# The last 16 channels' differences on 104 token rows, packed difference arrays, and a new order of work

## The chip, the cores and the metric

The kernel runs on one core of one Trainium2 chip. The metric is device time in microseconds (us): the median of several runs. The engines are PE (TensorE, matrix products; its weight loads are listed as PEld), DVE (VectorE), ACT (ScalarE), POOL (GpSimd) and SP (SyncE, which here only issues transfers). Each engine works through its own instructions in order and waits on semaphores.

## What is computed

A causal, dilated convolution of 15 taps over 2 sequences of 16,000 tokens with 144 channels, a gate, and a last projection:

```python
B, T, D, K = (2, 16000, 144, 15)          # x (B,T,D), w (K,D,2D), w_o (D,D), bf16
dil = 2
pad = (K - 1) * dil
xp = jnp.pad(x, ((0, 0), (pad, 0), (0, 0)))
h = jnp.einsum('btc,cd->btd', xp[:, pad:pad + T, :], w[0])
for i in range(1, K):
    off = pad - i * dil
    h = h + jnp.einsum('btc,cd->btd', xp[:, off:off + T, :], w[i])
f = h[..., :D]
g = h[..., D:]
z = jnp.tanh(f) * _sigmoid(g)
return z @ w_o
```

## The kernel before

**Windows and octets.** The tokens are cut into 16 windows of 2048 (WT), each with 32 tokens of history before it (WB = 2080). A window is worked in two octets, one for the even and one for the odd tokens (rho = 0, 1): 32 octets in all. An octet makes 8 outputs for each of 128 groups of 16 tokens. Sums of weights multiply x itself and differences of x are multiplied by single weights, so that products are shared between outputs.

**Leaves.** In an octet, A1, A2, A3, B1 and C1 are leaves: two products in common (`v` in the plan: vA1, vB ...), a copy by ACT to a second bank of PSUM (`k`: kA2, kB ...), then private products for each of two results (`p`: pA2_0, pA2_1 ...). `d` (dB_0 ...) copies a B or C result into one more bank, B2, B3, C2 and C3 add direct products. `a1s` copies A1's results to SBUF, `q` and `y` combine on DVE, `th` and `sg` are tanh and sigmoid on ACT, `m` multiplies them into z, `zt` transposes z by DMA, `g` is the output projection on PE, `po` its copy out by ACT, `ost` the store. PSUM has two banks for A, five for B and C, one for the projection.

**Differences.** From the transposed window xn (channels on partitions) DVE makes d2, d4, d8 (x at distance 2, 4, 8), d48 (of d4, at 8), d28 and d24 (of d2, at 8 and 4). Products read them with a step of 16 tokens (`st`, L246). In d8, d48 and d28 the runs that are needed alternate in sign, so each is made by two instructions, one for each sign (`sets_`, L117 to L122).

**The last 16 channels.** 144 channels are 128 and 16. For the last 16 the tokens are rearranged in DRAM (`gather`, L91: array xg, four arrays by the token's remainder modulo 4) and read back transposed with rows of 128 = 8 tokens x 16 channels that overlap (`remainder`, L101: tile rx), so that one product covers 8 tokens. DVE makes `re`, the difference of tokens 2 apart, from rx on all 128 partitions: two instructions of 2 x 513 elements a window (L125). rx serves A2 and A3, re serves B2, B3, C2, C3.

**The order.** PE, ACT, DVE and SP follow a plan written out by hand: `PLAN` lists the operations of one octet, with an offset in octets after the colon. An entry of octet n with offset a is issued in slot n + a, and within a slot in the plan's order. Entries for a window (differences, loads) come once in two octets. All transfers but the stores of results, and some at the start, are issued on SP in that order, so one that waits holds up those behind it. `late` holds operations of the first octet that are put in just before the first that needs them.

**The start and the end.** At the start 20 products of zeros run on PE, the first window and the weights are loaded (xn and the four pieces of w_all on SP; raw, the last 16 channels of w, and the gather of the first window on ACT's queue), and sums of weights are made: sm, ss, a1v, av and bc by DVE, bcv by PE with an identity matrix and a copy by ACT (`summed`, L196). s_r, ns_r, wo_p and we_r come from raw through a product with `swap`. At the end (`finish_early`, `finish`) the projections of the last three octets run, and the last z is transposed by PE.

## Time and profile before

| what | us |
|---|---|
| median of 3 runs | 342.88 (342.65 to 343.07) |
| the profiled execution | 342.56 |
| its span, first to last instruction | 340.8 |
| PE, DVE, ACT busy | 327.7, 302.0, 241.0 |
| mean granted TensorE clock | 0.99 |
| transfers | 143,110 packets, 38.32 MB |
| SP's waits for z before a transpose of it | 153.4 in 28 waits |

The profile lists each engine's busy time. A matrix product is shown with a duration of 0.286 us for 288 columns, but products overlap, so that PE's busy time is the time in which any runs. "x2" merges two neighbouring instructions into a row. Behind a row, in brackets, stands the idle time before it and what ended that.

### The profile page before, as it was taken

The numbers are of one execution on the slowest core, as the hardware profiler recorded it, in microseconds if no ns is written. First come the engines' busy times: TensorE is split into PE (matmuls) and PEld (weight loads), VectorE is DVE, ScalarE is ACT, GpSimd is POOL, SyncE is SP. The second block draws the span as 40 slices with busy tenths as digits, with TensorE's granted clock in tenths as the row PEclk, the third lists the DMA queues.
The fourth block names the chain that finished last, engine by engine and source line by source line (L and its number), as shares of the span: only waits on it lengthen the run. The fifth ranks groups of instructions, "written<-read, shape, count | busy, mean of one in ns | idle before, by whom it ended". The sixth has DMA issues, their size and how long they took to land.

```text
span 340.8 us, 7525 instructions
## 1 busy us (share of the span) xinstructions
PE 327.7 (96%) x2705; PEld 307.4 (90%) x2705; DVE 302.0 (89%) x726; ACT 241.0 (71%) x583; POOL 7.6 (2%) x22
## 2 busy tenths in 40 slices
PE   8679999999999999999999999999999999999983
PEld 3469999999999999999999999999999999999972
DVE  3889999999999999999999999998999999998662
ACT  1535787777778777777777777777777777787763
POOL 8000000000000000000000000000000000000000
PEclk9799999999999999999999999999999999999998
DMA  8872454466664465666566459657445666632313
GB/s 191 161 106 38 53 114 78 138 100 168 107 163 96 71 140 81 167 107 169 90 60 165 83 139 108 170 102 106 128 71 143 106 167 107 95 110 37 104 37 126
DMA packets 143110, 38.32 MB, mean 112 GB/s; under 512 B 138866, under 2 KB 141058, under 8 KB 143074
## 3 DMA queue, kind: packets, MB, share of 16 engines
q1 hardware_dynamic: 138286, 29.12, 49.0%
q10 hardware_dynamic: 4500, 8.66, 7.2%
q8 instruction: 21, 0.34, 0.4%
q14 instruction: 15, 0.12, 0.1%
q0 software_dynamic: 288, 0.07, 0.1%
HBM read 2.38 MB, written 10.30 MB: 37 GB/s over the span
## 4 chain that ended last, share of the span: by engine, by line
PE 92%; DMA 4%; DVE 1%; ACT 1%; issue 1%; SPq 0%; DVEq 0%; ACTq 0%
PE bc L244 57%; PE a L244 25%; PE po L369 4%; PE po L366 4%; DMA w_all<-in_w_dram 3%; DMA zt<-z 1%; SPq L88 0%; PE bc L366 0%; DVE d L122 0%; PE bc L200 0%; PE bc L369 0%; DVE q L305 0%; ACT a L270 0%; DVE re L132 0%; ACT th L332 0%
## 5 line engine op out<-in xcount | busy, mean ns | idle before, releaser
L244 PEld LDWEIGHTS <-d 128*128 128x128 bf16 x1856 | 231.8, 145 | 8.3 <-issue 2.7
L244 PE MATMUL bc<-w_all,d 128*128 128x288 bf16 x960 | 156.8, 286 | 1.9 <-DVE d L122 1.6
L327 DVE TENSOR_TENSOR y<-q,bc 128x288 f32<-128x288 f32 x256 | 113.6, 450 | 13.1 <-PE bc L244 10.4
L270 ACT COPY a<-a 128x288 f32<-128x288 f32 x96 | 36.8, 383 | 57.6 <-PE a L244 57.5
L305 DVE TENSOR_TENSOR q<-a1s,a 128x288 f32<-128x288 f32 x128 | 52.6, 451 | 13.1 <-PE a L244 11.1
L274 ACT COPY bc<-bc 128x288 f32<-128x288 f32 x128 | 50.8, 398 | 15.6 <-PE bc L244 14.6
L122 DVE TENSOR_TENSOR d<-d 128x516 bf16<-128x516 bf16 (+1 forms) x96 | 59.7, 668 | 0.0
L244 PE MATMUL a<-sm,d 128*128 128x288 bf16 x256 | 50.0, 287 | 0.8 <-ACT a L270 0.8
L244 PE MATMUL bc<-bc,d 128*128 128x288 bf16 x256 | 47.1, 286 | 0.1
L122 DVE TENSOR_TENSOR d<-xn 128x260 bf16<-128x260 bf16 (+2 forms) x64 | 42.6, 690 | 4.5 <-DMA xn<-in_x_dram 4.5
L332 ACT ACTIVATE sg<-y 128x576 bf16<-128x576 f32 x64 | 44.1, 689 | 1.0 <-DVE y L327 1.0
L332 ACT ACTIVATE th<-y 128x576 bf16<-128x576 f32 x64 | 43.7, 682 | 0.0
L359 ACT CAST o<-po 128x432 bf16<-128x432 f32 (+1 forms) x87 | 41.8, 481 | 0.8 <-PE po L369 0.8
L244 PE MATMUL bc<-wo_p,re 128*128 128x288 bf16 x128 | 36.6, 286 | 0.0
L244 PE MATMUL bc<-we_r,re 128*128 128x288 bf16 x128 | 36.6, 286 | 0.0
L339 DVE TENSOR_TENSOR z<-th,sg 128x512 bf16<-128x512 bf16 (+1 forms) x128 | 35.6, 301 | 0.0
L302 ACT COPY a1s<-a 128x288 f32<-128x288 f32 x64 | 25.9, 409 | 7.4 <-PE a L244 7.2
L369 PEld LDWEIGHTS <-zt 128*128 128x128 bf16 x256 | 22.8, 98 | 8.4
L369 PE MATMUL po<-wo_m,zt 128*128 128x144 bf16 x235 | 29.1, 226 | 0.0
L244 PEld LDWEIGHTS <-re 128*128 128x128 bf16 x256 | 28.8, 112 | 0.1
L366 PE MATMUL po<-wo_bd,zt 128*128 128x432 bf16 (+1 forms) x88 | 28.7, 326 | 0.0
L270 ACT COPY bc<-bc 128x288 f32<-128x288 f32 x64 | 25.8, 403 | 4.0 <-ACT a1s L302 2.2
(54 smaller groups left out, 228.6 us busy)
## 6 DMA issues: line engine op xcount, KB each, us to landing
out_dram<-o ACTq DMA_DIRECT2D x13, 576.0 KB
xg<-in_x_dram SPq DMA_DIRECT2D x28, 32.5 KB
w_all<-in_w_dram SPq DMA_DIRECT2D x3, 288.0 KB
out_dram<-o SPq DMA_DIRECT2D x1, 576.0 KB
zt<-z SPq DMA_TRANSPOSE x31
out_dram<-o ACTq DMA_DIRECT2D x1, 468.0 KB
out_dram<-o ACTq DMA_DIRECT2D x1, 288.0 KB
rx<-xg SPq DMA_TRANSPOSE x17
```

The lines of the kernel that those rows point to most:

```text
L122: nc.vector.tensor_tensor(out=o, in0=a, in1=b_, op=ALU.subtract)
L244: nc.tensor.matmul(ps[:, 0:D2], lhsT=l, rhs=r, start=start, stop=stop, skip_group_check=on)
L270: nc.scalar.copy(out=self.ts[1][:, 0:D2], in_=self.ts[0][:, 0:D2])
L274: nc.scalar.copy(out=self.other[i][:, 0:D2], in_=self.ts[i][:, 0:D2])
L302: nc.scalar.copy(out=self.get(cp_pool, "a1s", [P, 2, D2], F32)[:, i, :], in_=self.A1.ts[i][:, 0:D2])
L305: nc.vector.tensor_tensor(out=self.get(cp_pool, name, [P, 2, D2], F32)[:, i, :], in0=self.t["a1s"][:, i, :], in1=leaf.ts[i][:, 0:D2], op=op)
L327: nc.vector.tensor_tensor(out=y[:, k + 4 * i, :], in0=self.t[q][:, i, :], in1=ts[i][:, 0:D2], op=op)
L332: nc.scalar.activation(out=t[:], in_=self.t["y"][:, k::2, lo:lo + D], func=func)
L339: nc.vector.tensor_tensor(out=o, in0=th[:, :, lo:lo + n], in1=sg[:, :, lo:lo + n], op=ALU.mult)
L359: nc.scalar.copy(out=o, in_=a)
L366: nc.tensor.matmul(o.po[g][:, 0:n * D], lhsT=o.zt[:, 8, :], rhs=wo_bd[:, r0:r0 + n, :].rearrange("p r e -> p (r e)"), start=True, stop=False)
L369: nc.tensor.matmul(o.po[g][:, i * D:(i + 1) * D], lhsT=o.zt[:, r0 + i, :], rhs=wo_m[:], start=False, stop=i == n - 1)
```

## The change

- The last 16 channels are loaded as they lie, 20 tokens and 2 more on each of 104 partitions (`gather`, tile xt). ACT copies them (`rest`, plan entry `cr`) and DVE subtracts tokens 2 apart (`rest_diff`, `dr`), both ordered by the token's remainder modulo 4, into xs. Two transfers (`spread`, `wg`) write both to xg, and two transposes read them back as rx and re. DVE no longer makes re from rx.
- d4 and d48 are kept packed, two tokens of each four, and are read with a step of 8. The other derived arrays but d8 start two elements further on (`pad`). d8 and d28 are made by one instruction, with a zero step in one operand; d48 by two shorter-strided ones; d4 as one run.
- Half of bc (j = 0, 1) is summed on PE, with copies by ACT; DVE makes the other half. The first window's d48 comes after the third sum of weights. The first A2 uses the banks of B and C.
- The plan is another: among others d48 and d24 move from the slot before to the slot of their use, d2, d4 and d8 from two slots before to one, and the output's work (g, po) to an earlier slot.
- On ACT's queue at the start the first window's loads come ahead of raw.

```diff
 PLAN = """
-    pA3_1:0 xg:-2 sg0:1 m1a:2 d28:-1 kB:0 rx0:-1 po0:3 pB_0:0 m1b:2 th0:1 yC2_1:1 q3_0:0 C3_1:1 vA1:-1
-    q3_1:0 g1:3 dB_0:0 kA1:-1 pB_1:0 yC3_0:1 B2_0:0 yC3_1:1 d24:-1 pA1_0:-1 po1:3 g2:3 d2:-2 pA1_1:-1
-    yB2_0:0 zt:2 dB_1:0 a1s_0:-1 po2:3 d4:-2 vC:0 d48:-1 a1s_1:-1 ost:3 B3_0:0 B2_1:0 vA2:-1 kC:0
-    yB3_0:0 B3_1:0 yB2_1:0 pC_0:0 pC_1:0 kA2:-1 dC_0:0 pA2_0:-1 pA2_1:-1 m0a:1 C2_0:0 d8:-2 m0b:1
-    yB3_1:0 sg1:1 q2_0:-1 th1:1 xl:-3 dC_1:0 q2_1:-1 re:-1 C3_0:0 yC2_0:0 vA3:-1 vB:-1 C2_1:0 g0:2
-    kA3:-1 pA3_0:-1
+    a1s_1:0 xl:-1 dC_1:1 C3_0:1 d8:-1 kA2:0 d48:0 yC2_0:1 vB:0 xt:-2 rx:0 pA2_0:0 pA2_1:0 po2:3 ost:3
+    d24:0 d2:-1 q2_0:0 kB:0 C2_1:1 vA3:0 sg0:1 q2_1:0 yC3_0:1 wg:-1 pB_0:0 yC2_1:1 d28:-1 kA3:0 dB_0:0
+    C3_1:1 pB_1:0 yC3_1:1 d4:-1 th0:1 dB_1:0 re:0 cr:-2 pA3_0:0 sg1:1 q3_0:0 zt:2 m0a:1 pA3_1:0 B2_0:0
+    m0b:1 vC:0 yB2_0:0 th1:1 B3_0:0 B2_1:0 g0:2 kC:0 q3_1:0 vA1:-1 B3_1:0 kA1:-1 pC_0:0 dr:-2 po0:2
+    pC_1:0 pA1_0:-1 g1:2 yB2_1:0 m1a:1 dC_0:0 m1b:1 yB3_0:0 a1s_0:-1 pA1_1:-1 C2_0:0 yB3_1:0 vA2:-1
+    po1:2 g2:2
 """
...
+    NX = WB // 20
...
-    def gather(wi, halves=(0, 1), eng=nc.sync):
+    def gather(wi, eng=nc.sync):
...
+        xt = sets[wi]["xt"] = xt_pool.tile([NX, 22, CR], BF16, name="xt")
+
+        def part(p, e, t=0, te=22):
+            src = bass.AP(x.tensor, x.offset + (b * T + t0 - H + 20 * p + t) * D + CM, [[20 * D, e - p], [D, te - t], [1, CR]])
+            eng.dma_start(out=xt[p:e, t:te, :], in_=src)
+        if t0 == 0:
+            (nc.gpsimd if wi else nc.vector).memset(xt[0:2], 0.0)
+            part(2, 98)
+            part(98, NX)
+            part(1, 2, 12)
...
+        else:
+            part(0, NX)
+
+    def by_residue(wi, t):
+        return sets[wi]["xt"][:, t:t + 20, :].rearrange("p (j r) c -> p r j c", r=4)
+
+    def rest(wi):
+        xs = sets[wi]["xs"] = xt_pool.tile([NX, 2, 4, 5, CR], BF16, name="xs")
+        nc.scalar.copy(out=xs[:, 0], in_=by_residue(wi, 0))
+
+    def rest_diff(wi):
+
+        nc.vector.tensor_tensor(out=sets[wi]["xs"][:, 1], in0=by_residue(wi, 2), in1=by_residue(wi, 0), op=ALU.subtract)
+
+    def spread(wi, eng=nc.sync):
+
+        for q in (0, 1):
+            dst = bass.AP(xg.tensor, xg[wi, q, 0:1, 0:1].offset, [[5 * CR, NX], [NJ * CR, 4], [1, 5 * CR]])
+            eng.dma_start(out=dst, in_=sets[wi]["xs"][:, q].rearrange("p r j c -> p r (j c)"))
+
+    def remainder(wi, q):
+        name = ("rx", "re")[q]
+        t = sets[wi][name] = xa_pool.tile([P, WB], BF16, name=name)
+        nc.sync.dma_start_transpose(out=t[:], in_=bass.AP(xg.tensor, xg[wi, q, 0:1, 0:1].offset, [[CR, WB], [1, P]]))
+
+    half = {"d4", "d48"}
+    pad = {"x": 0, "d8": 0}
...
+                if name == "d4":
+                    forms = [((0, [[1, hi]]), (4, [[4, hi // 2], [1, 2]]), (0, [[4, hi // 2], [1, 2]]))]
+                elif first is None:
+                    forms = [((0, [[1, hi]]), (d, [[1, hi]]), (0, [[1, hi]]))]
+                else:
+                    e = d // (2 if name in half else 1)
+                    n = (hi - first - e - run) // (2 * e) + 1
+                    runs = [[2 * e, n], [1, run]]
+                    if run == e:
+                        forms = [((first, runs), (first, runs), (first + e, runs)), ((first + e, runs), (first + 2 * e, runs), (first + e, runs))]
+                    else:
+                        forms = [[(c, [runs[0], [k, 2], runs[1]]) for c, k in ((first, e), (first, 2 * e), (first + e, 0))]]
...
+        return dict(d4=sub("d4", "x", 4), d2=sub("d2", "x", 2), d8=sub("d8", "x", 8, 8, 2), d48=sub("d48", "d4", 8, 2, 4),
+                    d28=sub("d28", "d2", 8, 6, 4), d24=sub("d24", "d2", 4, 2, 4))
...
+    gather(0, nc.scalar)
     nc.gpsimd.memset(w_all[:, K, :], 0.0)
     raw = const.tile([P, 2, D2], BF16)
...
-    gather(0, (0,), nc.scalar)
-    gather(0, (1,), nc.scalar)
+    rest(0)
+    rest_diff(0)
+    spread(0, nc.scalar)
...
-    remainder(0, (0,))
-    remainder(0, (1,))
+    remainder(0, 0)
+    remainder(0, 1)
...
-    for k in ("d8", "d4", "d48"):
+    for k in ("d8", "d4"):
         pre0[k]()
...
+        if c == 2:
+            pre0["d48"]()
...
     raw_sums(0)
+    bc = const.tile([CM, 4, 2, D2], BF16, name="bc")
+    for j in (0, 1):
+        for e in (1, 0):
+            summed([(ident[:], wq[:, j, i, e, :]) for i in (0, 1)], [(bc[:, j, e, :], 1.0)])
     add(av[:], quad[:, :, 0], quad[:, :, 1])
     pre0["d2"]()
-    bc = const.tile([CM, 4, 2, D2], BF16, name="bc")
-    add(bc[:], wq[:, :, 0], wq[:, :, 1])
+    add(bc[:, 2:4], wq[:, 2:4, 0], wq[:, 2:4, 1])
     pre0["d28"]()
...
-    late = [(0, {"pA1_0", "pA1_1"}, lambda: raw_sums(1)), (0, directs, lambda: pre0["re"](slice(0, 1))), (0, directs, pre0["d24"]),
-            (1, directs, lambda: pre0["re"](slice(1, 2)))]
+    late = [(0, {"pA1_0", "pA1_1"}, lambda: raw_sums(1)), (0, directs, pre0["d24"])]
...
-            self.A2 = Leaf(s, True, "d4", "d48", rho - 4, lambda j: av[:, j, 1, :], lambda j, i: quad[:, j, i, 1, :],
+            self.A2 = Leaf(s, s is not sets[0] or rho > 0, "d4", "d48", rho - 4, lambda j: av[:, j, 1, :], lambda j, i: quad[:, j, i, 1, :],
...
+    fetch = dict(xt=gather, cr=rest, dr=rest_diff, wg=spread, rx=lambda wi: remainder(wi, 0), re=lambda wi: remainder(wi, 1))
```

More of the change, by code (lines that the diff above doesn't have):

```diff
@@ L56 @@
     NJ = WB // 4
-    HB = 2 * NJ + 16
+    NX = WB // 20
     assert T >= WT and T % 16 == 0
@@ L69 @@
     dram = ctx.enter_context(tc.tile_pool(name="dram", bufs=1, space=bass.MemoryType.DRAM))
+    xt_pool = ctx.enter_context(tc.tile_pool(name="xt", bufs=2))
     xd_pool = ctx.enter_context(tc.tile_pool(name="xd", bufs=2))
@@ L89, in load @@
         return dict(x=xn)
-    def gather(wi, halves=(0, 1), eng=nc.sync):
+    def gather(wi, eng=nc.sync):
         b, t0, _ = wins[wi]
-        lo = H if t0 == 0 else 0
-        for h in halves:
-            dst = xg[wi, h * HB:h * HB + 2 * NJ, :].rearrange("(k j) c -> j k c", k=2)
-            if lo:
-                eng.dma_start(out=dst[0:lo // 4], in_=zero[0:lo // 4, 0:2 * CR].rearrange("j (k c) -> j k c", c=CR))
-            eng.dma_start(out=dst[lo // 4:], in_=x[b, t0 - H + lo:t0 + WT, CM:D].rearrange("(j k h) c -> h j k c", k=2, h=2)[h])
@@ L101, in remainder @@
-    def remainder(wi, halves=None):
-        if "rx" not in sets[wi]:
-            sets[wi]["rx"] = xa_pool.tile([P, 2 * HB], BF16, name="rx")
-        for a, n in ((0, HB + 2 * NJ),) if halves is None else ((h * HB, 2 * NJ) for h in halves):
-            nc.sync.dma_start_transpose(out=sets[wi]["rx"][:, a:a + n],
-                                        in_=bass.AP(xg.tensor, xg[wi, a:a + 1, 0:1].offset, [[CR, n], [1, P]]))
+        xt = sets[wi]["xt"] = xt_pool.tile([NX, 22, CR], BF16, name="xt")
@@ new lines, in part @@
+        def part(p, e, t=0, te=22):
[6 more added lines that the diff above has]
+            part(1, 2, 12)
+        elif t0 + WT == T:
+            nc.gpsimd.memset(xt[96:NX, 20:22, :], 0.0)
+            part(0, 96)
+            part(96, NX - 1)
+            part(NX - 1, NX, 0, 20)
+        else:
+            part(0, NX)
@@ L108, in derive_steps, with sub @@
+    def remainder(wi, q):
[4 more added lines that the diff above has]
+    pad = {"x": 0, "d8": 0}
     def derive_steps(s):
         ahead = {"x": 0}
-        def sub(name, of, d, *sets_):
+        def sub(name, of, d, first=None, run=0):
             ahead[name] = ahead[of] + d
-            hi = WB - ahead[name]
+            hi = (WB - ahead[name]) // (2 if name in half else 1)
@@ L116, in go @@
             def go():
-                t = s[name] = xd_pool.tile([P, WB], BF16, name=name)
-                for first, step, inner, sign in sets_ or ((0, hi, [[1, hi]], 1),):
-                    count = (hi - first - 1 - sum(a * (n - 1) for a, n in inner)) // step + 1
-                    o, a, b_ = (bass.AP(t_.tensor, t_[:, first + off:first + off + 1].offset, [t_.ap[0], [step, count]] + inner)
-                                for t_, off in ((t, 0), (s[of], d if sign > 0 else 0), (s[of], 0 if sign > 0 else d)))
+                t, x = xd_pool.tile([P, WB], BF16, name=name), s[of]
@@ new lines, in go @@
+                s[name] = t
+                if name == "d4":
[10 more added lines that the diff above has]
+                        forms = [[(c, [runs[0], [k, 2], runs[1]]) for c, k in ((first, e), (first, 2 * e), (first + e, 0))]]
@@ L122, in go @@
+                for form in forms:
+                    o, a, b_ = (bass.AP(t_.tensor, t_[:, c + p:c + p + 1].offset, [t_.ap[0]] + dims)
+                                for (c, dims), t_, p in zip(form, (t, x, x), [pad.get(k, 2) for k in (name, of, of)]))
                     nc.vector.tensor_tensor(out=o, in0=a, in1=b_, op=ALU.subtract)
             return go
-        def re(h=slice(0, 2)):
-            if "re" not in s:
-                s["re"] = xd_pool.tile([P, 2 * HB], BF16, name="re")
-            o, a = (t[:].rearrange("p (h n) -> p h n", h=2)[:, h, 0:2 * NJ].rearrange("p h (k j) -> p h k j", k=2)
-                    for t in (s["re"], s["rx"]))
-            n = NJ - 7
-            for k in (0, 1):
-                nc.vector.tensor_tensor(out=o[:, :, k, 0:n], in0=a[:, :, 1 - k, k:k + n], in1=a[:, :, k, 0:n], op=ALU.subtract)
@@ L134, in derive_steps @@
-        pair, quads = [[1, 2]], [[1, 4]]
-        return dict(d4=sub("d4", "x", 4, (0, 4, pair, 1)), d2=sub("d2", "x", 2),
-                    d8=sub("d8", "x", 8, (0, 16, pair, 1), (8, 16, pair, -1)),
-                    d48=sub("d48", "d4", 8, (12, 16, [[4, 2]] + pair, 1), (4, 16, [[4, 2]] + pair, -1)),
-                    d28=sub("d28", "d2", 8, (14, 16, quads, 1), (6, 16, quads, -1)),
-                    d24=sub("d24", "d2", 4, (6, 8, quads, 1), (2, 8, quads, -1)), re=re)
+        return dict(d4=sub("d4", "x", 4), d2=sub("d2", "x", 2), d8=sub("d8", "x", 8, 8, 2), d48=sub("d48", "d4", 8, 2, 4),
+                    d28=sub("d28", "d2", 8, 6, 4), d24=sub("d24", "d2", 4, 2, 4))
@@ L169 @@
     s = {}
-    xg = dram.tile([NW, 2 * HB, CR], BF16, name="xg")
-    sets = [None] * NW
-    sets[0] = load(0)
+    xg = dram.tile([NW, 2, WB + 16, CR], BF16, name="xg")
+    sets = [{} for _ in range(NW)]
+    sets[0].update(load(0))
+    gather(0, nc.scalar)
     nc.gpsimd.memset(w_all[:, K, :], 0.0)
@@ L177 @@
     nc.scalar.dma_start(out=raw[0:P - CR, 1, :], in_=w[1:K:2, CM:D, :])
-    nc.scalar.dma_start(out=xg[:].rearrange("w (h n) c -> (w h) (n c)", h=2)[:, 2 * NJ * CR:], in_=zero[0:2 * NW, 0:CR * CR])
-    gather(0, (0,), nc.scalar)
-    gather(0, (1,), nc.scalar)
+    nc.scalar.dma_start(out=xg[:].rearrange("w q n c -> (w q) (n c)")[:, WB * CR:], in_=zero[0:2 * NW, 0:CR * CR])
+    rest(0)
+    rest_diff(0)
+    spread(0, nc.scalar)
     for c in range(0, 16, 4):
         nc.sync.dma_start(out=w_all[:, c:min(c + 4, K), :], in_=w[c:min(c + 4, K), 0:CM, :].rearrange("k c d -> c k d"))
-    remainder(0, (0,))
-    remainder(0, (1,))
+    remainder(0, 0)
+    remainder(0, 1)
     swap = const.tile([P, P], BF16)
@@ L234, with st @@
     raw_sums(0)
+    bc = const.tile([CM, 4, 2, D2], BF16, name="bc")
+    for j in (0, 1):
+        for e in (1, 0):
+            summed([(ident[:], wq[:, j, i, e, :]) for i in (0, 1)], [(bc[:, j, e, :], 1.0)])
     add(av[:], quad[:, :, 0], quad[:, :, 1])
     pre0["d2"]()
-    bc = const.tile([CM, 4, 2, D2], BF16, name="bc")
-    add(bc[:], wq[:, :, 0], wq[:, :, 1])
+    add(bc[:, 2:4], wq[:, 2:4, 0], wq[:, 2:4, 1])
     pre0["d28"]()
     directs = {"B2_0", "B2_1", "B3_0", "B3_1", "C2_0", "C2_1", "C3_0", "C3_1"}
-    late = [(0, {"pA1_0", "pA1_1"}, lambda: raw_sums(1)), (0, directs, lambda: pre0["re"](slice(0, 1))), (0, directs, pre0["d24"]),
-            (1, directs, lambda: pre0["re"](slice(1, 2)))]
+    late = [(0, {"pA1_0", "pA1_1"}, lambda: raw_sums(1)), (0, directs, pre0["d24"])]
     def mm(ps, l, r, start, stop, on=False):
         nc.tensor.matmul(ps[:, 0:D2], lhsT=l, rhs=r, start=start, stop=stop, skip_group_check=on)
-    def st(t, off):
-        c0 = H + off
-        return t[:, c0:c0 + 16 * (P - 1) + 1:16]
+    def st(s, name, off):
+        c0, step = H + off, 16
+        if name in half:
+            c0, step = c0 // 4 * 2 + c0 % 4, 8
+        c0 += pad.get(name, 2)
+        return s[name][:, c0:c0 + step * (P - 1) + 1:step]
     def st_r(t, off):
         q = off + 4
-        c0 = q % 2 * HB + q % 4 // 2 * NJ + q // 4
+        c0 = q % 4 * NJ + q // 4
         return t[:, c0:c0 + 4 * (P - 1) + 1:4]
@@ L265, in common @@
             for j in range(2):
-                mm(self.ts[0], st(self.s[sig], off - 16 * j), v(j), j == 0, j == 1)
+                mm(self.ts[0], st(self.s, sig, off - 16 * j), v(j), j == 0, j == 1)
         def copy(self):
@@ L278, in private @@
             for j in range(2):
-                mm(self.ts[i], st(self.s[dsig], off - 8 + 8 * i - 16 * j), f(j, 1 - i), False, rem is None and j == 1, True)
+                mm(self.ts[i], st(self.s, dsig, off - 8 + 8 * i - 16 * j), f(j, 1 - i), False, rem is None and j == 1, True)
             if rem is not None:
@@ L309, in direct @@
             for j in range(n):
-                mm(ts, st(self.s["d24"], off - 8 * j), f(j), False, False, True)
+                mm(ts, st(self.s, "d24", off - 8 * j), f(j), False, False, True)
             mm(ts, st_r(self.s[rsig], roff), rw, False, True, True)
@@ L383 @@
     live, outs = {}, {}
+    fetch = dict(xt=gather, cr=rest, dr=rest_diff, wg=spread, rx=lambda wi: remainder(wi, 0), re=lambda wi: remainder(wi, 1))
     def issue(n, name):
         wi, rho = octs[n]
-        if name == "xg":
-            gather(wi)
-            return
         if name == "xl":
-            sets[wi] = load(wi)
+            sets[wi].update(load(wi))
             sets[wi].update(steps=derive_steps(sets[wi]))
@@ L394, in issue @@
         s = sets[wi]
-        if name == "rx0":
-            remainder(wi)
+        if name in fetch:
+            fetch[name](wi)
             return
@@ L472 @@
     plan = [(t.split(":")[0], int(t.split(":")[1])) for t in PLAN.split()]
-    even = set(pre0) | {"xl", "xg", "rx0"}
+    even = set(pre0) | set(fetch) | {"xl"}
     outwards = {"g0", "g1", "g2", "po0", "po1", "po2", "ost"}
```

## The prediction

> **What bounds the kernel now.** I read the busy shares first, then the granted clock and busy times by stage, then the chain of waits, and last the timeline of the first 23 us and of the last 12 us.

> ```profile
> PE 327.7 (96%) x2705; PEld 307.4 (90%) x2705; DVE 302.0 (89%) x726; ACT 241.0 (71%) x583; POOL 7.6 (2%) x22
> ...
> 10.00:20.00 10.00, 6.82 (x38) 4.74 (x37) 7.70 (x16) 4.05 (x12) 0.00 (x0) 0.83 0.67 116
> 20.00:30.00 10.00, 8.39 (x69) 8.20 (x69) 9.36 (x21) 4.80 (x13) 0.00 (x0) 1.00 0.76 116
> ...
> 98.40:108.20 9.80, 9.80 (x85) 9.41 (x84) 9.20 (x23) 7.45 (x19) 0.00 (x0) 1.00 0.57 146
> ```

> After the times, a stage's row gives busy us (and instructions) of PE, PEld, DVE, ACT and POOL, then clock, DMA share and GB/s. In the steady stretch PE is busy 9.80 of 9.80 us at clock 1.00; DVE has 0.6 us to spare, ACT 2.3.

> ```profile
> 40.83 1.35 PE bc L244 x11
> ...
> 50.64 1.35 PE bc L244 x11
> ...
> 60.45 1.35 PE bc L244 x11
> ```

> The chain of waits repeats every 9.81 us: one octet. From the code an octet is 72 matmuls of 288 columns plus, for the output, 3 of 432, 432 and 288 and 8 of 144: 83 matmuls, 23,040 columns, 0.426 ns a column, some 0.122 us for one of 288. The change alters none of these 83. So what it takes off DVE can be worth nothing in the steady stretch, about 300 of the 340.8 us, and I look for the difference at the two ends.

> ```profile
> 5.56 0.65 ACTq L99 DMA_DIRECT2D xg<-in_x_dram  x1
> 7.59 0.59 ACTq L99 DMA_DIRECT2D xg<-in_x_dram  x1
> 12.39 0.28 PE L244 MATMUL a<-a1v,xn 128*128 128x288 bf16 x1 [2.17 <-DVE a1v L142]
> 15.55 0.38 ACT L270 COPY a<-a 128x288 f32<-128x288 f32 x1 [0.31 <-PE a L244]
> 19.65 0.76 DVE L132 TENSOR_TENSOR re<-rx 128x513 bf16<-128x513 bf16 x2
> 20.32 1.30 DVE L122 TENSOR_TENSOR d<-d 128x1036 bf16<-128x1036 bf16 x2
> 21.68 0.59 PE L244 MATMUL bc<-w_all,d 128*128 128x288 bf16 x3 [1.61 <-DVE d L122]
> ```

> At the start PE reaches its first direct products (B2_0) only at 21.68 us, when DVE has done re and then both parts of d24; from there it hardly stops. This moment, T, is what the change can move.

> ```profile
> 332.44 0.36 PE L366 MATMUL bc<-wo_bd,zt 128*128 128x432 bf16 x1 [0.80 <-DMA zt<-z]
> ...
> 333.43 0.44 PE L353 MATMUL a<-ident,z 128*128 128x128 bf16 x5
> ```

> At the end PE waits 0.80 us for the transposed z of octet 30, and the last transposes, whose z was ready at 332.76, stand behind it until 333.43.

> **The change, steady stretch.** Per window (two octets, 19.62 us) DVE loses two re of 0.693 and gains one difference of 320 elements on 104 partitions. No row has that form; it lies between z of 64 elements (0.184) and re of 513 (0.424): I take 0.33. d48 now reads and writes runs of four at half the stride, as d24 does (1036 elements in 0.698), so its two parts lie between 0.35 and the 0.605 of now: 0.40. d8 in one instruction lies between 0.40 (half of d4, 1038 elements in 0.699) and 0.73 (the pair of now): 0.60. d28 in one lies between 0.65 and 1.20: 1.05. DVE saves about 1.0 + 0.4 + 0.15 + 0.15 = 1.7 us a window; ACT gains a copy of 320 elements, between 0.383 (288) and 0.588 (512): 0.42. Both are hidden under PE.

> What could uncover them is the new order: d48 and d24 are now made in the slot that uses them, not the slot before. I walked one pair of slots, PE at full rate, y and q at 0.40 (two of them take 0.81). In the odd slot DVE does d8, d2, d28 and d4 (3.5 us) besides 16 smaller operations and comes to yB3_1 about 1.3 us before the slot ends; d48 (0.8) is then done 0.5 us before the even slot begins, and pA2_0 wants it 0.86 us after. d24 ends at 1.4, B2_0 is at 4.3. The tightest is ACT's kA2, 0.3 us ahead of pA2_0. So: no stall, 0.

> Transfers: one more transpose of 2080 rows a window (re comes by DMA now), 832 packets of 160 bytes to spread, 2288 short packets for 2080. Queue 1 took 138,286 packets, some 8,640 a window, with a share of 49%; some 3,100 more make 66%. On SP the order becomes xt, rx, re, zt, xn, two spreads, zt. The spreads wait for ACT's copy and DVE's difference, with the next zt, rx and re queued behind them; but the difference is made at 0.6 of an even slot, that zt is ready at 0.75, and rx and re are wanted over a slot later. Cost 0; if that cover of about 7 us went, pA2 would be late next.

> **The start.** Three things change. (1) On ACT's queue the loads of xt (three issues) come first, raw's second half must wait until xn has landed, and then come the copy (0.42) and two spreads (about 0.6 each by the 0.59 and 0.65 above). In the trace of before the 5.56 issue is one that waited for xn, so xn lands at about 5.5; with xt's 2254 packets ahead I say 6.3, bounded by 5.5 and 7.6. raw's second half, then issued at 6.3, took 5.4 us from its issue at 2.19 to the wait that ended at 7.59, while the DMA share was over 1.1; from 8 us on that load drains. I bound its flight by 2.0 (the zeros, issued at 3.60, had let the next go by 5.56) and 5.0 and take 3.0, near the lower, because the w_all chunks are mostly through: PE's first real sums start at 9.3 instead of 8.13. (2) ACT's chain from there: 0.45 to the first sum, four copies 1.2, two bcv 0.74, four new copies for bc 1.48, kA1 0.38, two bcv 0.74, two a1s 0.88, kA2 0.38: 6.25, so kA2 ends at about 15.5 against 15.93. The new copies take nearly all that an empty ACT had (2.20 us idle before 12.71). The 8 new matmuls (8 x 0.12 = 0.98 us) fall in PE's idle 2.17 us. (3) DVE does half of bc, 0.75 by av's row of equal size for 1.35, and no re: it is through d28 at about 15.8, not 16.49.

> Then from kA2's end at 15.5: two products and a remainder 0.37 and 0.17 until the result is seen; meanwhile A3's common products, kB and kA3 on ACT to about +1.55; pA3_0 +2.1; q3_0 +2.5; first half of d24 +3.15, and B2_0 needs only that half. T = 18.7 at full clock. rx must land before kA2 ends: xs is copied at about 8.2, spread by 8.8, landed at 11; the transpose issued at 10.52 was used at 16.17, so 5.6 bounds its flight from above and 2.0 from below; I take 4.5, 15.5, just in time. re, a transpose later, lands by 17.5.

> The clock is the disputed part. By rows of one us the granted clock was 0.66, 0.50, 0.50, 0.63 from 13 to 17, after PE had been idle for 2.2 us. If the same happens, the three pieces above that are PE's (eight products, 0.98 us) double, some 0.9 us: T = 19.6. I take that value, since PE's early work is again thin. Two octet-1 products that were made before T now come after: +0.25. The start gives 21.68 - 19.6 - 0.25 = 1.8 us; bounds 0.4 (raw's half 1.4 later) and 2.7 (no halving).

> [...]

> **The end.** z of octet 30 is multiplied before the last y, not after: its transpose (3.24 us from issue to use) starts about 1.5 us earlier against the last products, so the wait of 0.80 goes and the last transposes stand at 332.76, 0.65 earlier. ACT's sg and th of octet 30 also stand before kC, where PE lost 0.23 at 327.38 and 0.2 at 328.86. I take 0.8, bounds 0.2 and 1.1.

> **Sum.** 340.8 - 1.8 - 0.8 = 338.2 span. The profiled execution took 342.56, 1.76 around its span, and the median is 0.32 above it: 338.2 + 1.76 + 0.32 = 340.3.

> **Rivals.** (a) The start's new serial chain (xn, then raw, then ACT) eats its gain: if raw's flight is 5.0 us, kA2 ends at 17.5 and T is 21.6 at half clock, a start of -0.2 and with the end 0.6 us in all: 342.3. For it: DMA shares of 1.1 to 1.3 up to 10 us. Against: raw no longer meets xn. (b) Slower: even slots stall, as d48 and d24 are made in the slot of their use. The place is pA2_0 and B2_0 of octets 2, 4, ... 30. Each has 1.3 us of lead or more in my walk; it decides once DVE is later than that, and it pays back the 2.6 us as soon as a stall is over 0.17 us in each of the 15 even slots. DVE one y (0.45) later than that lead is 15 x 0.45 = 6.7 us: 347.0. For it: in the trace DVE's busy share is 93%. Against: DVE drops to about 85%, and the odd slot of before held more difference work (5.0 us) without a stall. (c) The start's differences were never the limit, something else (rx or re landing at 21) holds T, and the end alone moves: 342.1.

> **How the numbers follow.** Forecast 0.66, (a) 0.12, (b) 0.11, (c) 0.11. About 0.2%, 0.7 us, is what a measurement of this kernel can tell from no change. The bounds of start and end together give 342.9 - 3.8 = 339.1 to 342.9 - 0.6 = 342.3; (a) and (c) lie at that upper end, and with 0.3 us for the measurement on either side the range is 338.8 to 342.6, which leaves out (b) and the far ends. Faster by over 0.2% (below 342.2): the forecast but for its far end, half of (c), a third of (a): 0.75; within: the rest, 0.14; slower: (b), 0.11.

> **What would show it.** B2_0's first product at 19 to 20.5 us, not 21.68; the octet's period still 9.81 with PE's busy time equal to the stage; DVE's share in the steady stretch near 85%; raw's second issue only after xn; no wait on zt in the last 12 us. It is wrong if the period grows, if PE waits for DVE's d in the steady stretch, or if T stays above 21.

## The result, and the profile after

The changed kernel takes 341.11 us (median of 6 runs, 341.04 to 341.14), the kernel before, run beside it, 342.69 (342.06 to 343.07). The ratio is 0.9955 with a 95% interval of 0.9942 to 0.9968: faster by 0.45%. 340.3 was predicted, with a range of 338.8 to 342.6. The profiled execution took 341.14 around a span of 339.4.

The busy shares of the changed kernel, with its first DMA queue, and a steady stage (busy us and instructions of PE, PEld, DVE, ACT and POOL, then granted clock, DMA share, GB/s):

```profile
PE 326.8 (96%) x2713; PEld 307.7 (91%) x2713; DVE 271.4 (80%) x677; ACT 250.2 (74%) x603; POOL 8.2 (2%) x25
...
q1 hardware_dynamic: 187600, 39.67, 65.9%
```

```profile
98.40:108.20 9.80, 9.80 (x85) 9.42 (x84) 8.37 (x21) 7.79 (x20) 0.12 (x1) 1.00 0.72 124
```

DVE lost 30.6 us of work (302.0 before), and in the steady stretch PE is as full as it was. The chain of waits of the changed kernel, first at the start, then in the steady stretch:

```profile
3.71 6.00 DMA xt<-in_x_dram
...
9.82 0.06 DVE xs L122
...
10.07 1.15 DVE d L164 x2
...
15.11 0.32 DVE a1v L171
...
15.47 0.28 PE a L279
...
20.73 0.70 DVE d L164
...
21.48 0.59 PE bc L279 x3
```

```profile
98.25 1.84 PE bc L279 x15
...
108.07 1.84 PE bc L279 x15
...
117.89 1.84 PE bc L279 x15
```

The period is 9.82 us, as before (9.81). But T, the start of B2_0, is 21.48 where 19.6 was forecast and 21.68 stood before. The chain says why: it begins with the landing of xt and then runs through DVE. The timeline of the same stretch shows the queue behind that landing (after the start and duration: engine, line, operation, and in brackets the idle time before it):

```profile
6.03 0.79 ACTq L207 DMA_DIRECT2D raw<-in_w_dram  x1
...
9.82 0.33 DVE L122 TENSOR_TENSOR xs<-xt 104x320 bf16<-104x320 bf16 x1 [8.47 <-DMA xt<-in_x_dram]
10.07 1.15 DVE L164 TENSOR_TENSOR d<-xn 128x516 bf16<-128x516 bf16 x2
...
10.46 0.28 PE L231 MATMUL bc<-raw,swap 128*128 128x288 bf16 x1 [2.25 <-DMA raw<-in_w_dram]
11.12 0.45 DVE L171 TENSOR_TENSOR sm<-w_all 128x576 bf16<-128x576 bf16 x1
11.30 0.53 PE L231 MATMUL bc<-raw,swap 128*128 128x288 bf16 x3 [0.56 <-DMA raw<-in_w_dram]
...
15.47 0.28 PE L279 MATMUL a<-a1v,xn 128*128 128x288 bf16 x1 [1.55 <-DVE a1v L171]
```

raw's second issue stands at 6.03; in the run of the late difference, below, DVE's wait for xn ends at 5.97, beside that issue at 5.96, so xn was there at about 6.0. d8 and d4, which need only xn, start at 10.07, because DVE stood 8.47 us for xt. In the kernel before, DVE went from xn straight to the differences and the sums:

```profile
5.64 1.30 DVE L122 TENSOR_TENSOR d<-xn 128x260 bf16<-128x260 bf16 x3 [4.47 <-DMA xn<-in_x_dram]
...
8.04 0.45 DVE L142 TENSOR_TENSOR sm<-w_all 128x576 bf16<-128x576 bf16 x1
```

So the first sum of weights begins at 11.12 (8.04 before), and PE gets its second product with a1v at 15.47 (12.39 before). T came only 0.20 us earlier than before, and that is about what the start gained: at the first products of octet 31 that wait for a copy by ACT, PE is 0.14 us ahead of before.

At the end, the kernel before:

```profile
327.38 0.65 PE L244 MATMUL bc<-w_all,d 128*128 128x288 bf16 x4 [0.23 <-ACT bc L274]
...
328.40 0.40 ACT L274 COPY bc<-bc 128x288 f32<-128x288 f32 x1
328.48 0.29 PE L244 MATMUL bc<-we_r,re 128*128 128x288 bf16 x1
...
328.86 0.65 PE L244 MATMUL bc<-w_all,d 128*128 128x288 bf16 x4
```

and the changed kernel:

```profile
326.31 0.52 DVE L377 TENSOR_TENSOR z<-th,sg 128x512 bf16<-128x512 bf16 x2
...
326.80 0.87 ACT L312 COPY bc<-bc 128x288 f32<-128x288 f32 x2 [1.28 <-PE bc L279]
326.90 1.29 SPq L381 DMA_TRANSPOSE zt<-z  x1
...
327.24 0.65 PE L279 MATMUL bc<-w_all,d 128*128 128x288 bf16 x4 [0.23 <-ACT bc L312]
...
328.33 0.29 PE L279 MATMUL bc<-we_r,re 128*128 128x288 bf16 x1
...
328.46 0.65 PE L279 MATMUL bc<-w_all,d 128*128 128x288 bf16 x4
...
330.96 0.35 PE L404 MATMUL bc<-wo_bd,zt 128*128 128x432 bf16 x1
...
332.20 0.53 PE L391 MATMUL a<-ident,z 128*128 128x128 bf16 x5
```

Two things changed here. Before, the products at 328.86 followed those at 328.48 by 0.38 us, just behind a copy by ACT that ended at 328.80; now the same pair is 0.13 apart, since ACT had made both copies at once at 326.80. That is a gain of 0.25, and the first of the closing projections stands at 329.68 (330.08 before). The transpose of octet 30's z is issued at 326.90 (329.15 before), PE goes into its projection at 330.96 without a wait, and the last transposes stand at 332.20 (333.43 before). From 329.68 to the span's end it is 9.7 us, against 10.7 before: a gain of 1.0. So of the 1.4 us that the span lost, 0.15 came from the start and 1.25 from the end.

### The profile page after: what moved, and what is told of

Its sections match the earlier page's. It is cut to its first block, busy times and chain, and to the rows that moved or that the text cites. A ratio compares the mean times of both kernels' runs of the same rounds, so it can differ in the third digit from the quotient of the medians.

```text
span 339.4 us, 7548 instructions
## 1 busy us (share of the span) xinstructions
PE 326.8 (96%) x2713; PEld 307.7 (91%) x2713; DVE 271.4 (80%) x677; ACT 250.2 (74%) x603; POOL 8.2 (2%) x25
## 3 DMA queue, kind: packets, MB, share of 16 engines
q1 hardware_dynamic: 187600, 39.67, 65.9%
## 4 chain that ended last, share of the span: by engine, by line
PE 92%; DVE 2%; DMA 2%; issue 1%; ACT 1%; ACTq 0%; DVEq 0%
PE bc L279 58%; PE a L279 25%; PE po L407 4%; PE po L404 4%; DMA xt<-in_x_dram 2%; DVE d L164 1%; DVE sm L171 0%; DVE o L399 0%; DVE ss L171 0%; PE bc L231 0%; DVE z L377 0%; ACTq L99 0%; PE bc L404 0%; DVE a1v L171 0%; ACT L185 0%
## 5 line engine op out<-in xcount | busy, mean ns | idle before, releaser
L365 DVE TENSOR_TENSOR y<-q,bc 128x288 f32<-128x288 f32 x256 | 112.0, 451 | 43.7 <-PE bc L279 43.6
L343 DVE TENSOR_TENSOR q<-a1s,a 128x288 f32<-128x288 f32 x126 | 54.2, 450 | 8.9 <-ACT bc L308 3.9
L279 PE MATMUL a<-sm,d 128*128 128x288 bf16 x252 | 48.9, 286 | 0.0
L164 DVE TENSOR_TENSOR d<-d 128x516 bf16<-128x516 bf16 (+2 forms) x80 | 44.1, 585 | 0.0
L308 ACT COPY bc<-bc 128x288 f32<-128x288 f32 x65 | 25.2, 389 | 21.5 <-PE bc L279 12.7
L164 DVE TENSOR_TENSOR d<-xn 128x516 bf16<-128x516 bf16 (+2 forms) x48 | 41.0, 857 | 0.0
L377 DVE TENSOR_TENSOR z<-th,sg 128x512 bf16<-128x512 bf16 (+1 forms) x128 | 33.3, 302 | 0.0
```

What stands on the lines that cost most here:

```text
L164: nc.vector.tensor_tensor(out=o, in0=a, in1=b_, op=ALU.subtract)
L279: nc.tensor.matmul(ps[:, 0:D2], lhsT=l, rhs=r, start=start, stop=stop, skip_group_check=on)
L308: nc.scalar.copy(out=self.ts[1][:, 0:D2], in_=self.ts[0][:, 0:D2])
L343: nc.vector.tensor_tensor(out=self.get(cp_pool, name, [P, 2, D2], F32)[:, i, :], in0=self.t["a1s"][:, i, :], in1=leaf.ts[i][:, 0:D2], op=op)
L365: nc.vector.tensor_tensor(out=y[:, k + 4 * i, :], in0=self.t[q][:, i, :], in1=ts[i][:, 0:D2], op=op)
L377: nc.vector.tensor_tensor(out=o, in0=th[:, :, lo:lo + n], in1=sg[:, :, lo:lo + n], op=ALU.mult)
```

## Experiments

Each kernel is the changed one with the edit shown. The kernel before, run beside them, took 342.42 (25 runs) for the first four, 342.34 (21 runs) for the next four and 342.26 (7 runs) for the last three. T is the start of the first product with d24. Theory D: DVE standing still for xt sets the start. Theory A: raw and ACT's copies behind it do.

**The difference later on DVE.** DVE forms xs's difference behind the first two pieces of weights; its spread and the two transposes go out on SP behind it.

```diff
     rest(0)
-    rest_diff(0)
-    spread(0, nc.scalar)
+    spread(0, nc.scalar, (0,))
...
             add(a1v[:, c // 2, :], ss[:, c - 1, :], ss[:, c, :])
+        if c == 1:
+            rest_diff(0)
+            spread(0, nc.sync, (1,))
+            remainder(0, 0)
+            remainder(0, 1)
```

> DVE makes the first window's difference of the last 16 channels behind the first two pieces of weight sums instead of ahead of everything; its transfer and the two transposes follow it. Theory D (DVE, in order, stands still until xt lands at 9.8 us, and d8, d4 and the weight sums behind it set the start): PE's second product with a1v comes at about 12.5 us, not 15.47; ACT's chain from raw then limits (kA1 at about 14.8, not 15.8), T about 20.5 and the time about 1.0 us shorter, 340.1. Theory A (raw and ACT's chain set the start): a1v comes earlier, but T stays at about 21.5 and the time at 341.1.

339.67 us (339.40 to 341.00, 9 runs), ratio 0.992 (0.9896 to 0.9944). Its timeline:

```profile
5.97 1.15 DVE L164 TENSOR_TENSOR d<-xn 128x516 bf16<-128x516 bf16 x2 [4.62 <-DMA xn<-in_x_dram]
...
7.10 0.46 DVE L171 TENSOR_TENSOR sm<-w_all 128x576 bf16<-128x576 bf16 x1
...
9.85 0.33 DVE L122 TENSOR_TENSOR xs<-xt 104x320 bf16<-104x320 bf16 x1
...
11.11 0.53 PE L228 MATMUL bc<-raw,swap 128*128 128x288 bf16 x3 [0.31 <-DMA raw<-in_w_dram]
...
19.23 1.31 DVE L164 TENSOR_TENSOR d<-d 128x1036 bf16<-128x1036 bf16 x2
...
19.98 0.59 PE L281 MATMUL bc<-w_all,d 128*128 128x288 bf16 x3 [0.79 <-DVE d L164]
```

xt lands no earlier (9.8) and raw no earlier (11.1), yet d8 starts 4.1 us and T comes 1.5 us sooner: D. Six runs, at a mean clock of 0.994 to 0.999, took 339.40 to 339.70; the three at 0.990 took 340.66 to 341.00, which matters below. The gain, 1.4 us, is more than theory D's 1.0.

**raw ahead of xt on ACT's queue.** The edit moves `gather(0, nc.scalar)` behind the two loads of raw.

> raw is issued ahead of xt on ACT's queue, as in the kernel before; the difference stays ahead of all on DVE. Theory D: raw lands by 8.5, but a1v still waits for DVE, which waits for xt: T stays within 0.5 us of 21.5, time 340.7 to 341.6. Theory A: PE's first real sums start at about 8.5 instead of 11.3, T falls by more than 1 us, time below 340.2.

345.71 us, ratio 1.0092 (1.0062 to 1.0123), T at 26.71. Timeline:

```profile
3.06 5.57 ACTq L99 DMA_DIRECT2D xt<-in_x_dram  x3
...
8.31 0.65 PE L231 MATMUL bc<-raw,swap 128*128 128x288 bf16 x4
...
12.96 0.33 DVE L122 TENSOR_TENSOR xs<-xt 104x320 bf16<-104x320 bf16 x1 [11.61 <-DMA xt<-in_x_dram]
...
18.59 0.40 PE L279 MATMUL a<-a1v,xn 128*128 128x288 bf16 x1 [1.23 <-DVE a1v L171]
```

raw is there three us earlier (four products at 8.31) and it helps nothing, because xt lands three us later (12.96). DVE waits for it, and so does ACT, whose copy of xs stands ahead of ns_r: PE stood 5.11 us, until 15.04, for a bank that ACT had to empty. The clock then was 0.50 from 13.7 to 23.9, so the 4.6 us above the changed kernel are not xt's lateness alone. Both theories missed the size, since both took xt's landing as nearly fixed. The run speaks against A as it was put, since an early raw alone shortened nothing, but it does not separate DVE's wait from ACT's.

**Both edits at once.**

> Both edits together. Theory D with A as the next limit: T about 19.5, time about 339.2, more than the first edit alone gives. Theory D alone: the same as with the first edit alone. Theory A alone: the same as with raw first alone. If rx or re holds T, 340 or more.

343.32 us, ratio 1.002 (1.0002 to 1.0037), T at 23.85: a miss for every expectation. The late xt (12.74) held ACT as in the run before: its copy of xs stands ahead of ns_r and of the copies of bcv and bc, PE stood 4.89 us until 14.38 for a bank that ACT had to empty, and the clock was 0.50 from 12.6 to 19.5. So the wait for xt costs on ACT as on DVE, since both have work for the sums of weights behind it: PE's 4.89 us here, DVE's 8.47 in the changed kernel.

**All of bc on DVE again**, as in the kernel before.

```diff
-    for j in (0, 1):
-        for e in (1, 0):
-            summed([(ident[:], wq[:, j, i, e, :]) for i in (0, 1)], [(bc[:, j, e, :], 1.0)])
...
-    add(bc[:, 2:4], wq[:, 2:4, 0], wq[:, 2:4, 1])
+    add(bc[:], wq[:, :, 0], wq[:, :, 1])
```

> All of bc is made by DVE again, as in the kernel before; the rest is the changed kernel. Theory D: DVE's chain sets the start and gets 0.6 us longer (1.35 for 0.75), T about 22.0, time 341.6. Theory A: ACT's chain is four copies (1.38 us) shorter, T up to 1 us earlier, time 340.2 to 340.6.

342.6 us (341.20 to 343.08, 10 runs), ratio 0.9999 (0.9978 to 1.0020); T at 22.61 in the profile, in which the granted clock was 0.50 from 16 to 19. The median does not tell the whole: the two runs at a mean clock of 0.998 took 341.20 and 341.33, within 0.2 of the changed kernel, the eight at 0.987 to 0.994 took 342.4 to 343.1. So bc on PE saves next to nothing as long as the clock holds, and 1.3 us or more where it falls. That fits PE's idle time, 2.16 us before its second product with a1v where the changed kernel has 1.55, but what makes the clock fall was not tried here.

**d24 early.** On top of the late difference, `pre0["d24"]()` stands behind d28, no longer in `late`.

> The late difference of the first experiment, and d24 of window 0 made right behind d28 instead of behind the first half of q3. In the run of the late difference DVE was idle for 1.05 us before q2 (17.26) and then made d24 only at 19.23, so that PE stood 0.79 us for it until T = 19.98, while its products before it were through at 19.19. Theory D (DVE's order at the start sets T): d24 is done at about 17.5, q2 comes 0.26 later, B2_0 follows the last product of A3 at once: T about 19.2, time about 338.9, some 0.8 below the late difference alone. Rival (the landing of re holds B2's remainder, or the later q2 holds a bank): PE then stands for re or for a bank near 19.5 to 20.4 and the time is again 339.5 to 339.8.

339.25 us (339.05 to 339.95, 4 runs), ratio 0.9913 (0.9899 to 0.9927): between the two expectations. In the profiled run (339.95, the slowest) PE's clock was 0.50 from 11.6 to 15.0, T was 20.35, and PE did not wait for d24. The others have spans of 337.2 to 337.5 at a clock of 0.994 to 0.996, against 338.2 at 0.992.

**z of octet 30 late, as before.** The two multiplications of octet 30 stand behind the first y of C of octet 31 again.

```diff
-    todo = sorted((n + at, n > 1 and n + at < 0, i, n, name) for i, (name, at) in enumerate(plan) for n in range(NO)
+    def held(n, name):
+        return n == NO - 2 and name in ("m1a", "m1b")
+
+    todo = sorted((n + at + held(n, name), n > 1 and n + at < 0, 7.5 if held(n, name) else i, n, name) for i, (name, at) in enumerate(plan) for n in range(NO)
```

> The changed kernel with one thing set back: the two multiplications of octet 30's z stand behind the first y of C of octet 31 on DVE, as they stood in the kernel before, and its transpose is issued after them. Theory E (the end's gain comes from the earlier z of octet 30): the transpose is issued 1.8 to 2.2 us later, PE waits 0.5 to 0.9 us for zt near 332, the last transposes stand behind it, and the time is 341.7 to 342.1, 0.6 to 1.0 above the changed kernel. Rival F (the end's gain comes from ACT, whose sigmoid and tanh of octet 30 stand ahead of the last copy): no wait on zt, time 341.1 as the changed kernel.

342.12 us (341.94 to 342.21, 11 runs): 1.0 above the changed kernel. Timeline of the end:

```profile
328.44 0.52 DVE L377 TENSOR_TENSOR z<-th,sg 128x512 bf16<-128x512 bf16 x2
...
329.02 1.29 SPq L381 DMA_TRANSPOSE zt<-z  x1
...
332.27 0.36 PE L404 MATMUL bc<-wo_bd,zt 128*128 128x432 bf16 x1 [1.13 <-DMA zt<-z]
...
333.27 0.44 PE L391 MATMUL a<-ident,z 128*128 128x128 bf16 x5
```

The wait is back (1.13, more than the 0.5 to 0.9 expected), and the last transposes stand behind it at 333.27. Theory E holds, with the time at the upper edge. The closing projections begin at 329.70, as in the changed kernel, so the 0.25 us of ACT's copies is not part of this 1.0.

**Spare work on DVE.** One, then two subtractions of 2078 elements (1.23 us each) into a tile that nobody reads, ahead of d48 in every even octet from octet 2 on; the diff shows the first, the second has `range(2)`.

```diff
             def go():
+                if name == "d48" and s is not sets[0]:
+                    for _ in range(1):
+                        nc.vector.tensor_tensor(out=spare[:, 0:2078], in0=s["x"][:, 2:2080], in1=s["x"][:, 0:2078], op=ALU.subtract)
                 t, x = xd_pool.tile([P, WB], BF16, name=name), s[of]
```

> The changed kernel with one more subtraction of 2078 elements (1.23 us, into a tile that nobody reads) on DVE just ahead of d48 in each even octet from octet 2 on: about what DVE was spared a window. Theory H (DVE's savings are hidden under PE, and d48 has a lead): d48 is made at 111.55 to 112.31 of the profile and first used at 114.29, a lead of 2.0 us, so nothing stalls: period 9.82, time 340.9 to 341.4, DVE's share back at about 86% of the span. Rival B (an even slot stalls as soon as DVE is later): each even slot loses up to 1.2 us, time up to 359; a loss of 0.1 us a slot would already show as 342.6.

341.74 us (341.56 to 341.87, 10 runs), 0.3 above theory H's range. 18.5 us more on DVE cost 0.6. The period is still 9.82, and nearly the whole cost is one wait, in octet 2:

```profile
37.70 0.41 PE L283 MATMUL a<-av,d 128*128 128x288 bf16 x2 [0.58 <-DVE q L347]
```

> The same with two such subtractions, 2.46 us ahead of d48. Theory H: the lead of 2.0 us is used up, PE waits for d at the first product with d48 in each even octet, by 0.4 to 0.5 us: 15 x 0.45 = 6.8, time 346 to 350. If instead the lead is shorter than the profile shows (the 1.3 us of the prediction), 15 x 1.15 = 17 us, 358. If nothing depends on d48's place, 341.2.

358.37 us. The waits of PE and the timeline of one even octet:

```profile
PE a L283 <- DVE q L347: 10.6, 15, 0.7
```

```profile
119.76 0.21 PEld L283 LDWEIGHTS <-d 128*128 128x128 bf16 x2 [0.25 <-DVE d L167]
...
120.32 1.29 DVE L167 TENSOR_TENSOR d<-d 128x1036 bf16<-128x1036 bf16 x2
...
121.54 0.81 DVE L347 TENSOR_TENSOR q<-a1s,a 128x288 f32<-128x288 f32 x2
122.04 0.41 PE L283 MATMUL a<-av,d 128*128 128x288 bf16 x2 [0.71 <-DVE q L347]
```

Even octets take 10.9 us, odd ones 9.82. The expectation was wrong in the place of most of it. For d48 only the weight load of pA2_0 waits (119.76), which costs PE some 0.2 us; the rest, 0.9, is for q2. q2 empties one of the two banks of A that A3's products need, and it stands behind d24 on DVE. 2.46 us more made 1.09 of stall, so the slack of an even slot is 1.37 us.

**The same with d24 behind q2.** In the plan d24:0 stands behind q2_1:0.

> Two spare subtractions ahead of d48 in every even octet (2.46 us, as in the run that took 358.37), with d24 moved behind both parts of q2 on DVE. In that run PE did not wait for d but 15 times for q2 (10.6 us in all), which stood behind d24 on DVE and held the bank that A3's common products need. Theory Q (the slot's slack ends at q2, 1.37 us after the normal time of DVE, and d24 ahead of it takes 1.3 of it): q2 comes about 1.2 us earlier, the waits for q2 go, the loss falls from 17 us to under 4: 341.1 to 345. Rival (d48's own lead, or the copies on ACT behind the late y, set the loss): 355 to 358 again.

347.22 us, ratio 1.0133 (1.0103 to 1.0162). The waits for q are gone, and with them 11.1 of the 17.3 us that the two subtractions had cost. What is left, 6.1 us, is above the expectation. Part of it is the wait for d48 at the weight load of pA2_0, which the run before has too (waits of PEld: us in all, times, longest):

```profile
PEld L283 <- DVE d L167: 5.8, 16, 1.2
```

Fifteen of the 16 are at pA2_0, 0.25 us each but for 1.18 in octet 2; the other is at T. A pair of octets takes 19.99 us for 19.64: some 0.2 of the 0.35 goes at pA2_0, and 0.13 at B2_0 (120.29), which follows a copy of B's result by ACT that came late (until 120.24).

**raw's products later, and more zeros at the start.** Both on top of the early d24: the first moves the four products with raw and their copies behind the sums of w_all; the second has NWARM = 28.

> The late difference and the early d24, and the four products with raw and their copies moved behind the sums of w_all on PE and ACT. In the run of the early d24 PE stood 3.11 us for raw (until 10.55), its clock fell to 0.50 from 11.8 to 15, its first product of A2 came at 17.95 (16.45 without that halving) and T was 20.35. Theory A2 (once DVE no longer waits for xt, raw's landing ahead of everything on PE and ACT is next, with the halved clock behind it): PE starts on w_all at about 8.6, has no idle time over 1.5 us, the clock stays at 1.00, kA1 is made at 13.9, T at 19.0 to 19.4, time 338.2 to 338.9. Rival (the remainder's path by xt, xs, rx and re is next, since rx landed at 16.8 there): PE waits for rx at its first product with it, T about 19.9, time 339.2.

339.24 us (338.97 to 339.41, 4 runs), ratio 0.9897 (0.9863 to 0.9932). T is 19.70; PE waited neither for raw nor for rx, but the clock fell all the same. Rows of one us, from 10 to 15:

```profile
10.00:11.00 1.00, 0.08 (x1) 0.00 (x0) 0.97 (x4) 0.57 (x3) 0.00 (x0) 1.00 0.46 79
11.00:12.00 1.00, 0.94 (x6) 0.54 (x6) 0.54 (x3) 1.00 (x4) 0.00 (x0) 1.00 0.77 130
12.00:13.00 1.00, 0.35 (x2) 0.21 (x2) 0.93 (x4) 1.00 (x5) 0.00 (x0) 1.00 0.00 0
13.00:14.00 1.00, 0.90 (x5) 0.55 (x5) 1.00 (x3) 1.00 (x4) 0.00 (x0) 0.58 0.00 0
14.00:15.00 1.00, 1.00 (x6) 0.65 (x5) 1.00 (x2) 0.43 (x2) 0.00 (x0) 0.50 1.01 214
```

The rival's time (339.2) came out, but not its reason, the wait for rx. In the profiled run the halved clock stands in the way of theory A2; but the run at a mean clock of 0.998, which leaves at most some 1.4 us at half clock (0.002 of 337.5 us, twice), less than any fall seen here (3.4 us or more), took 339.32, so the clock is not shown to be what held the gain back, and what did stays open.

> The late difference and the early d24, with 28 products of zeros at the start in place of 20, so that PE is idle for 1.5 us at most before raw lands instead of 3.1. Theory C (the halved clock from 11.8 to 15 cost the run of the early d24 about 1.1 us): the clock stays at 1.00 from 9 to 20, T is 19.2 to 19.5, time 338.2 to 338.8. Rival (the halving falls into time in which PE would wait anyway, as in the changed kernel, whose runs at 0.990 and 0.998 mean clock are equally long): T about 20.3, time 339.25.

338.96 us (338.74 to 339.79, 4 runs), ratio 0.9896 (0.9865 to 0.9928). In its profile the clock is 1.00 from 9 to 20, T is 19.11 and the span 337.2. Three runs at 0.994 to 0.996 have spans of 337.0 to 337.2, the one at 0.991 has 338.0. If that one had the halving, it costs about 0.9 us here, near theory C's 1.1, and the zeros do not always prevent it; only the first run has a trace. The medians of this kernel and the one with the early d24 alone can't be told apart (the intervals overlap). Its median is the lowest of the study, some 2 us below the changed kernel.

## Why the forecast fell short of its sum

| term | predicted | measured | shown by |
|---|---|---|---|
| steady stretch | 0 | 0 (9.82 a period) | the chain; one spare subtraction |
| T | 19.6 | 21.48 | the late difference |
| start in all | 1.8 | 0.15 | the profiles |
| end | 0.8 | 1.25 | the late z (1.0); the profiles |
| span | 338.2 | 339.4 | |
| around the span; median against the profiled run | 1.76; +0.32 | 1.74; -0.03 | |

**The steady stretch** was right. DVE's savings were worth nothing; DVE fell to 84% of the stretch from 100 to 200 us ("near 85%") and queue 1 rose to 65.9% ("66%"). From 31 to 324 us DVE's share went from 92.7% to 83.2%, which is 1.9 us a window of 19.6, not 1.7, mainly because d28 in one instruction (1032 elements) took 0.693, not 1.05: with its zero step it costs no more than a part of d24 (1036 elements, 0.698 before). d48's parts took 0.423 (0.40), d8 0.641 (0.60), the difference 0.319 (0.33).

**The start** was wrong, by the prediction's own sign (T above 21) and by its bounds (0.4 to 2.7). One step of it failed: "xs is copied at about 8.2", with what stood around it. The prediction asked what queues behind the transfers on ACT and SP, but not what is queued behind xs's difference on DVE: d8, d4, and all of sm, ss and a1v. It put xt into the flight of xn and raw and gave xt itself no price; its three issues took until 4.55 and it landed at 9.78. The wait moved DVE's whole chain by 3 us, and the prediction's own "DVE through d28 at 15.8" became 18.5. Taking the difference out of DVE's way gave T = 19.98. That it is close to 19.6 is partly luck: 19.6 held 0.9 for a halved clock, which that trace does not have, and without it the working says 18.7. A second term was mis-sized beside it: raw's second half, whose flight was taken as 3.0, took 5.3 us from its issue to its first product (6.03 to 11.30), just over the upper bound of 5.0. It was hidden behind DVE here; with the late difference it is on the path (PE's first sums at 10.5 and 11.1). The reason given for 3.0, that the load drains from 8 us on, is not in the rows of the kernel before: the DMA share was 1.29 from 8 to 9 and 1.09 from 9 to 10, and 0.39 only after that.

**The clock.** No halving was seen at the start in the profile of the changed kernel, after 2.25 us of idle PE. It comes and goes between executions: the changed kernel's runs at a mean clock of 0.990 and of 0.998 have spans of 339.3 alike. There the halving is free, since PE waits for DVE's sums anyway. The run of the late z, which has the same start, shows it in a trace: the clock was 0.50 from 12.0 to 15.4, and T was 21.50. The 0.9 us put down for it was the right size for a start in which PE is on the path (some 0.8 to 1.3, an estimate from the spread of the runs with the late difference), the wrong one for this start. The kernel before does pay: its runs at 0.997 to 0.999 took 341.5 to 342.1, those at 0.990 about 342.1 to 342.6. So against a run of the kernel before that looks unhalved (about 341.8) the change is worth some 0.7 us, less than the end's 1.25 alone. By that estimate the changed start is some 0.5 us longer than an unhalved start of before; that it comes out even is the halving that no longer costs. No trace of an unhalved run of the kernel before is there to confirm it.

**The end** was right in mechanism and 0.45 too small, above its upper bound of 1.1. The earlier z gave 1.0 for about 0.65. Of the two waits for ACT's copies, the 0.23 at 327.38 stayed (0.23 at 327.24) and the one at 328.86 went, which gave 0.25. The order on ACT as its cause is read from the two profiles; no run set it back alone.

**Luck.** The start fell short of its bounds and the end went over its own; that the sum of the two lies inside the range is partly that they err in opposite directions.

**The rivals.** (a) named raw and ACT and a T of 21.6; T came out at 21.48, but for another reason, as raw landed no earlier in the run that reached 19.98. (b) did not happen: an even slot has 1.37 us of slack (1.3 was walked). When two spare subtractions used it up, the wait was mostly for q2, which (b) did not name, and only some 0.2 us at pA2_0, which it did; the price was 1.09 us times 15. (c) fell: in the changed kernel neither PE nor its weight loads waited for rx or re.

## What to carry to other kernels

When an operation that waits for a new transfer is put into an engine's order, price the transfer's landing first, then write down everything behind it on that engine that does not need it; here an operation of 0.33 us held up everything behind it by 3 us. A late, small piece of work belongs behind what its engine can already do, even if it feeds a long path. The 30.6 us of work taken from DVE beside a full PE (9.80 of 9.80 us busy) were worth nothing by themselves, the period being 9.82 us for 9.81; an earlier pair of multiplications at the end, where PE otherwise waits 1.13 us for the transfer behind it, was worth 1.0 us.

## What the hardware showed that was not expected

Order on one queue moved landings by about 3 us: with raw's two issues ahead of it, xt's first issue came 2.1 us later (3.06 for 0.92) and the end of its last 4.1 us later (8.63 for 4.55), and it landed 3.1 us later, at 12.96; raw, issued at 0.92 and 2.19 instead of 4.58 and 6.03, was in use at 8.31, both halves of it, instead of 11.30.
